# Padding two short contractions with zero rows so that they span as many partitions as their neighbours

## The chip, the cores and the metric

The kernel runs on one core of one Trainium2 chip. The metric is the device time of one execution in microseconds (us); the time of a kernel is the median of its runs. A profiled execution gives the trace, whose span (first to last instruction) is a little shorter than the device time of that execution. Engines: PE is TensorE's matmul stream, PEld its weight loads, DVE is VectorE, ACT is ScalarE, POOL is GpSimd, SP issues the DMAs.

## The reference

Eight batches of eight heads of attention, with 512 local tokens and 32 global tokens, feed a two-layer MLP with a Mish activation. Local queries see the globals and a window of 32 keys on either side; global queries see all keys.

```python
k_all = np.concatenate([k_g, k_l], axis=2)
v_all = np.concatenate([v_g, v_l], axis=2)
out_g = np.matmul(sm(scale * q_g @ k_all.T), v_all)
mask = np.abs(pos[:, None] - pos[None, :]) <= 32
s_l = np.concatenate([scale * q_l @ k_g.T, np.where(mask, scale * q_l @ k_l.T, -1e9)], axis=-1)
out_l = np.matmul(sm(s_l), v_all)
x = concatenate([out_g, out_l], axis=2).transpose(0, 2, 1, 3).reshape(B * S, H * D)
h = x @ w_in
return (h * np.tanh(softplus(h))) @ w_out
```

## The kernel before, in words

A unit of attention is one batch `b`, one pair of heads `hp` (4 pairs) and one tile `t` of 128 local queries (4 tiles), so there are 128 units. For a unit, `scores` (L595 to L607) multiplies queries with the keys of the window, `row_max` and `expo` make the softmax numerators, `p_hi` and `p_lo` split them into two half-precision parts in `ph`, and `p_turn` transposes `ph` by DMA into `pt`, in which the keys lie on the partitions. `pv` (L646) then multiplies `pt`, the stationary operand, with the values, the moving operand of 64 columns. Every product of two split numbers takes three matmuls (high with high, high with low, low with high). For each of two heads the keys come in two chunks: the first against `va`, the second against `vc`, so a unit has 2 x 2 x 3 = 12 matmuls into the tile `U`. How many keys (rows of both operands) a chunk has stands in the table `CHK`, by `t`: 96 and 96, 128 and 96, 128 and 96, 128 and 64.

The global queries are done once for each pair of heads, 32 times in all. `g_scores`, `g_max`, `g_exp`, `g_norm` and `g_turn` lead to the transposed numerators `gpt`; `g_pv` (L737) multiplies them in five chunks of keys with three matmuls each, 15 in all, into the tile `gu`. The first chunk holds the 32 globals, in the partitions 96 to 127 of `va` and `gpt`; the other four hold 128 local keys each, from `vf`.

`v_move` copies the split values from `vf` and `vgf` into `va` and `vc` by seven DMAs for each pair of heads. `vc` has two buffers of [96, 4, 2, 128]; its rows 64 to 95 are written for `t` 0 to 2 only. `ph` and `gph` are tiles that are kept over the whole program (`kept`, L264): POOL fills them with zeros at the start, and two or one of them are used in turn.

Beside attention runs the MLP: `m1_mm` (L787, tile `h`) and `m2_mm` (L855, tile `o`), with Mish and the split of its result (tiles `e`, `G`) on ACT and DVE between them. There are 17 blocks of 256 tokens with 8 steps each. `slot(u)` puts the work of one attention unit and of one MLP step together. At the start the weights are unpacked and scaled (`w_load`, `w_sum`, `w_stat`, `w_split`). The order of the instructions on each engine is set by the planner `Plan`, which simulates the tasks with given costs and takes, on each engine, the one that can begin first. The costs handed over for `pv` and `g_pv` are by counts and columns, `mm(12, 69)` and `mm(15, 69)`, not by rows.

Of the kernel before, what the change touches and what calls it, by code (L numbers as in the profile page):

```python
# [12 lines left out]
F16 = mybir.dt.float16  # L13
# [27 lines left out]


WIN = [(0, 192, 32), (128, 224, 0), (288, 224, 0), (448, 192, 0)]
CHK = [(96, 96), (128, 96), (128, 96), (128, 64)]
GC = 64


# [167 lines left out]
def attn_mish_kernel(ctx: ExitStack, tc: tile.TileContext, qt, kt, qt0, kt0, vm, vg, qg, w1, w2, consts_in, out, w64):  # L215
    nc = tc.nc
    V, A, T, G = nc.vector, nc.scalar, nc.tensor, nc.gpsimd
# [16 lines left out]
    X = pl.tile  # L234

    def rings(pool, *table):
        for tag, bufs, shape, dt in table:
# [8 lines left out]

          ("qs", 2, [128, 2, SL], F32R), ("ks", 2, [128, 2, KW], F32R), ("kl", 2, [128, 2, KW], F32R),
          ("qgh", 2, [128, 3, HP, 64], F32R), ("vgf", 2, [128, 2, 128], F16),
          ("vf", 2, [128, 4, 2, 128], F16), ("va", 2, [128, 4, 2, 128], F16), ("vc", 2, [96, 4, 2, 128], F16),

          ("P", 3, [128, 2, 224], F32), ("nm", 6, [128, 1], F32), ("sums", 3, [128, 4, 2], F32), ("rs", 2, [128, 4, 2], F32),
          ("pt", 2, [128, 8, 128], F16), ("x", 1, [128, 4, 2, 64], F32), ("xs", 1, [128, 2, 4, 128], F16),
# [9 lines left out]
          ("u", 1, [128, 4, 2, 64], F32))  # L262


    def kept(tag, bufs, shape):
        tiles = [const.tile(shape, F16, name=f"{tag}{n}") for n in range(bufs)]
        for x in tiles:
            G.memset(x, 0.0)
        pl.ring(tag, bufs, lambda name, it=itertools.cycle(tiles): next(it))

    kept("ph", 2, [128, 2, 2, 256])
    kept("gph", 1, [64, 2, 640])


    def mm(n, cols):
        return n * max(27, cols / 2.4)
# [25 lines left out]
    def scaled(e, dst, src, c):  # L302

        if e == ACT:
            A.activation(out=dst, in_=src, func=AF.Copy, scale=c)  # L305
        else:
            V.tensor_scalar(dst, src, c, None, ALU.mult)  # L307
# [270 lines left out]
    def bank(name):  # L578

        return [("h" if early else "sc", name)]  # L580
# [66 lines left out]
    def pv(b, hp, t):  # L647
# [3 lines left out]
        def go():  # L651
            for h in range(2):
                n = 0
                for c, vx in ((0, va), (1, vc)):
                    k = CHK[t][c]
                    for p, vl in ((0, 0), (0, 1), (1, 0)):
# [78 lines left out]
    def g_pv(b, hp):  # L735
        pt, vf, va, u = ("gpt", b, hp), ("vf", b, hp), ("va", b, hp), ("gu", b, hp)

        def go():
            n = 0
            for c in range(5):  # L740
                r = slice(0, 128) if c else slice(96, 128)
                vv = X[vf][:, c - 1] if c else X[va][r, 1]
                for p, vl in ((0, 0), (0, 1), (1, 0)):
                    T.matmul(X[u][:, :64], vv[:, vl, :], X[pt][r, p * 5 + c, :], start=(n == 0), stop=(n == 14))  # L744
                    n += 1
        pl.add(PE, mm(15, 69), go, r=[pt, vf, va], new=bank(u))
        for h in range(2):
            r = slice(64 * h, 64 * h + 64)
            pl.add([(ACT, 200), (DVE, 158)], 0, lambda e, r=r, h=h: scaled(e, xg[r, hp, b * SG:(b + 1) * SG], X[u][r, 32 * h:32 * h + 32],
                                                                          X["sv", b][r, 2:3]), r=[u, ("sv", b)], w=[["xg", (b, hp, h)]])  # L750
# [305 lines left out]
    for x in ORDER.split():  # L1056
        a, n = x[0], int(x[1:] or 0)
# [87 lines left out]
```

## Time and profile before

| quantity | value |
|---|---|
| median of 3 runs | 1034.23 us (1033.37 to 1034.86) |
| profiled execution | 1032.9 us, span 1031.1 us |
| PE busy | 944.5 us, 92% of the span, 7906 matmuls |
| PEld busy | 670.3 us, 65% |
| ACT busy | 681.1 us, 66% |
| DVE busy | 665.0 us, 64% |
| POOL busy | 81.8 us, 8% |

The busy time is an average over three stages: the preparation of the weights together with the first units of attention, the long middle in which attention and the MLP run side by side, and the tail in which only the MLP is left. The time that a group of matmuls takes is read from the start of the group to the start of what follows, since the matmuls are pipelined and the duration of each is longer than its distance to the next.

### The profile page before, as it was taken

The numbers are of one execution on the slowest core, as the hardware profiler recorded it, in microseconds if no ns is written. First come the engines' busy times: TensorE is split into PE (matmuls) and PEld (weight loads), VectorE is DVE, ScalarE is ACT, GpSimd is POOL, SyncE is SP. The second block draws the span as 40 slices with busy tenths as digits, with TensorE's granted clock in tenths as the row PEclk, the third lists the DMA queues.
The fourth block names the chain that finished last, engine by engine and source line by source line (L and its number), as shares of the span: only waits on it lengthen the run. The fifth ranks groups of instructions, "written<-read, shape, count | busy, mean of one in ns | idle before, by whom it ended". The sixth has DMA issues, their size and how long they took to land.

```text
span 1031.1 us, 20578 instructions
## 1 busy us (share of the span) xinstructions
PE 944.5 (92%) x7906; PEld 670.3 (65%) x7906; DVE 665.0 (64%) x1704; ACT 681.1 (66%) x1321; POOL 81.8 (8%) x60
## 2 busy tenths in 40 slices
PE   3456797899999999999999999999999999999996
PEld 2234475566776777777767777777777777666663
DVE  6877896887667766776676666767676655422221
ACT  3465566666887788778878788787878788311110
POOL 2725222410000000000000000000000000000000
PEclk9999998999999999999999999999999999999998
DMA  9847983696758764766566665665576444100000
GB/s 333 220 115 171 281 233 78 121 187 155 165 105 176 144 143 105 182 141 141 116 163 148 131 131 129 159 128 133 119 162 125 116 75 79 38 11 21 1 21 21
DMA packets 231802, 134.65 MB, mean 131 GB/s; under 512 B 197528, under 2 KB 209048, under 8 KB 230680
## 3 DMA queue, kind: packets, MB, share of 16 engines
q1 hardware_dynamic: 231704, 133.34, 56.6%
q8 instruction: 62, 1.02, 0.4%
q14 instruction: 36, 0.29, 0.1%
HBM read 63.55 MB, written 8.91 MB: 70 GB/s over the span
## 4 chain that ended last, share of the span: by engine, by line
PE 71%; DVE 11%; DMA 7%; issue 2%; ACT 2%; SPq 1%; POOL 0%; ACTq 0%; DVEq 0%
PE o L855 29%; PE h L787 29%; PE U L657 4%; PE s L606 4%; DMA vraw<-in_vm 3%; PE g L695 2%; PE gu L744 2%; DMA gpt<-gph 2%; DVE vmx L479 1%; DMA pt<-ph 1%; DVE ph L640 1%; DVE P L612 1%; DVE ks L300 1%; DVE kl L544 1%; DMA wraw<-in_w 1%
## 5 line engine op out<-in xcount | busy, mean ns | idle before, releaser
L855 PE MATMUL o<-W,G 128*128 128x512 f16 x1632 | 389.9, 379 | 0.0
L787 PE MATMUL h<-xh,W 128*128 128x256 f16 x2048 | 379.3, 275 | 5.2 <-ACT e L830 5.1
L787 PEld LDWEIGHTS <-W 128*128 128x128 f16 x3264 | 310.9, 98 | 69.8 <-issue 5.5
L787 PE MATMUL h<-xl,W 128*128 128x256 f16 x1024 | 281.0, 274 | 0.0
L855 PEld LDWEIGHTS <-G 128*128 128x128 f16 x1632 | 156.8, 98 | 144.3 <-issue 0.3
L830 ACT ACTIVATE e<-h,c 128x512 f32<-128x512 f32 (+1 forms) x137 | 92.6, 683 | 117.0 <-PE h L787 115.9
L621 ACT ACTIVATE P<-P,nm 128x192 f32<-128x192 f32 (+1 forms) x256 | 117.8, 460 | 40.3 <-DVE nm L612 39.0
L612 DVE CUSTOM_DVE_ANT_0 P<-s,consts 128x192 f32<-128x192 f32 (+1 forms) x256 | 90.1, 367 | 79.3 <-PE s L606 70.2
L307 DVE TENSOR_SCALAR G<-e,c 128x512 f16<-128x512 f32 x129 | 63.2, 490 | 115.3 <-ACT e L830 115.1
L640 DVE SCALAR_TENSOR_TENSOR ph<-P,ph 128x384 f16<-128x384 f32 (+1 forms) x128 | 79.1, 619 | 82.0 <-ACT ph L305 81.3
L843 DVE SCALAR_TENSOR_TENSOR G<-e,c,G 128x512 f16<-128x512 f32 (+1 forms) x137 | 102.0, 744 | 3.4
L830 ACT ACT_TABLE_LOAD x79 | 101.4, 1283 | 1.4
L621 ACT ACT_TABLE_LOAD x74 | 94.9, 1283 | 1.4
L657 PEld LDWEIGHTS <-pt 96*128 96x128 f16 (+2 forms) x1536 | 64.1, 101 | 34.2 <-DMA pt<-ph 21.6
L305 ACT ACTIVATE ph<-P 128x384 f16<-128x384 f32 (+1 forms) x128 | 69.7, 547 | 16.3 <-DMA pt<-ph 13.2
L657 PE MATMUL U<-va,pt 128*128 128x64 f16 (+1 forms) x768 | 62.0, 200 | 14.8 <-DMA pt<-ph 12.5
L606 PE MATMUL s<-ks,qs 128*128 128x192 f32 (+1 forms) x216 | 71.4, 353 | 1.4 <-DVE qs L536 0.8
L657 PE MATMUL U<-vc,pt 96*128 96x64 f16 (+1 forms) x768 | 61.3, 198 | 0.0
L393 POOL TENSOR_TENSOR W<-W,wr 128x512 int32<-128x512 int32 x32 | 50.2, 1579 | 77.3 <-DVE W L391 42.4
L716 ACT ACTIVATE gP<-g,gmx 64x288 f32<-64x288 f32 x64 | 30.4, 476 | 37.8 <-DVE gmx L711 37.6
L606 PE MATMUL s<-kl,qs 128*128 128x192 f32 (+1 forms) x216 | 54.2, 274 | 0.0
L403 PE MATMUL ws<-W 128*128 128x128 bf16 x128 | 17.7, 285 | 37.0 <-POOL W L393 37.0
(102 smaller groups left out, 1016.6 us busy)
## 6 DMA issues: line engine op xcount, KB each, us to landing
kraw<-in_kt SPq DMA_DIRECT2D x27, 640.0 KB, 4.7
qraw<-in_qt SPq DMA_DIRECT2D x27, 512.0 KB, 4.1
W<-in_w SPq DMA_DIRECT2D x19, 512.0 KB, 6.1
out<-ob SPq DMA_DIRECT2D x34, 256.0 KB, 2.6
vraw<-in_vm SPq DMA_DIRECT2D x8, 1024.0 KB, 6.1
wraw<-in_w SPq DMA_DIRECT2D x13, 512.0 KB, 6.2
vc<-vf SPq DMA_DIRECT2D x32, 128.0 KB, 2.3
va<-vf SPq DMA_DIRECT2D x32, 96.0 KB, 2.3
```

The lines of the kernel that those rows point to most:

```text
L305: A.activation(out=dst, in_=src, func=AF.Copy, scale=c)
L307: V.tensor_scalar(dst, src, c, None, ALU.mult)
L393: pl.add(POOL, pool(512), lambda: G.tensor_tensor(f(), f(), X["wr", k], ALU.add), r=[("wr", k)], w=[key])
L606: T.matmul(X[s][:, :w], X[qs][:, h, t * 128:(t + 1) * 128], X[k][:, h, c0:c0 + w], start=(i == 0), stop=(i == 1))
L612: pl.add(DVE, 69 + 1.04 * w, lambda: V.tensor_tensor_reduce(out=X[P][:, h, :w], in0=X[s][:, :w], in1=mask[:, m0:m0 + w], scale=-SCALE, sca ...
L621: pl.add(ACT, 160 + 0.832 * w + 93, lambda: A.activation(out=X[P][:, h, :w], in_=X[P][:, h, :w], func=AF.Exp, bias=X[nm], scale=-1.0, accu ...
L640: pl.add(DVE, dve(n), lambda: V.scalar_tensor_tensor(p_part(X[ph], t, 1), p_src(X[P], t), PSC, p_part(X[ph], t, 0), ALU.mult, ALU.subtract ...
L657: T.matmul(X[u][:, t, h, :], X[pt][:k, p * 4 + h * 2 + c, :], X[vx][:k, t, vl, h * 64:(h + 1) * 64], start=(n == 0), stop=(n == 5))
L787: T.matmul(X[h][:, f * TB:(f + 1) * TB], wh(i, wl)[:, off:off + 128], X[x][:, d, o:o + TB], start=(n == 0), stop=(n == 11))
L830: chain(blk, i, ACT, 571, lambda a, z: A.activation(out=X[e][:, a:z], in_=hv(blk, i)[:, a:z], func=AF.Mish, bias=0.0, scale=X[c][:, 0:1]), ...
L843: chain(blk, i, DVE, 602, lambda a, z: V.scalar_tensor_tensor(gp(1, blk, i)[:, a:z], X[e][:, a:z], X["c", blk][:, 2:3], gp(0, blk, i)[:, a ...
L855: T.matmul(X[o], gp(g, blk, i)[:, f, t * 128:(t + 1) * 128], wh(8 + i, wl)[:, f * 512:(f + 1) * 512], start=(i == 0 and n == 0), stop=(i = ...
```

## The change

The second chunk of the last query tile has 96 rows in place of 64, and the globals' chunk of `g_pv` has 128 rows in place of 32. For the first, the two buffers of `vc` become kept tiles which POOL fills with zeros at the start: rows 64 to 95 of the last query tile's part are never written by a DMA and stay zero. For the second, the columns 0 to 95 of `gph`, which stay zero, become the rows 0 to 95 of the first chunk of `gpt`, and they multiply whatever values stand in those rows of `va`.

```diff
-CHK = [(96, 96), (128, 96), (128, 96), (128, 64)]
+CHK = [(96, 96), (128, 96), (128, 96), (128, 96)]
...
-          ("vf", 2, [128, 4, 2, 128], F16), ("va", 2, [128, 4, 2, 128], F16), ("vc", 2, [96, 4, 2, 128], F16),
+          ("vf", 2, [128, 4, 2, 128], F16), ("va", 2, [128, 4, 2, 128], F16),
...
     kept("ph", 2, [128, 2, 2, 256])
+    kept("vc", 2, [96, 4, 2, 128])
     kept("gph", 1, [64, 2, 640])
...
             for c in range(5):
-                r = slice(0, 128) if c else slice(96, 128)
-                vv = X[vf][:, c - 1] if c else X[va][r, 1]
+                vv = X[vf][:, c - 1] if c else X[va][:, 1]
                 for p, vl in ((0, 0), (0, 1), (1, 0)):
-                    T.matmul(X[u][:, :64], vv[:, vl, :], X[pt][r, p * 5 + c, :], start=(n == 0), stop=(n == 14))
+                    T.matmul(X[u][:, :64], vv[:, vl, :], X[pt][:, p * 5 + c, :], start=(n == 0), stop=(n == 14))
```

The order of the instructions on PE, DVE, ACT and SP is the same in both kernels, and so is their number. On POOL two instructions are new, at the start of the program. This is what stands there before; `ph` and `gph` are the kept tiles, and `p` is the result of the first reduction over the partitions, for the scale of the values:

```order
L268 MEMSET ph_72 128x1024
L268 MEMSET ph_73 128x1024
L268 MEMSET gph_76 64x1280
L490 ISA
L490 ISA p_0_151<-vmx_123 128x1
L393 ISA
```

And this is what stands there in the changed kernel, at the same place on POOL:

```order
L269 MEMSET ph_72 128x1024
L269 MEMSET ph_73 128x1024
L269 MEMSET vc_76 96x1024
L269 MEMSET vc_77 96x1024
L269 MEMSET gph_80 64x1280
L492 ISA
L492 ISA p_0_155<-vmx_127 128x1
L395 ISA
```

The two fills of `vc` stand behind those of `ph` and ahead of that of `gph` and of the first reduction.

## Rows read from the trace of the kernel before

**Rows 1.** The page, busy time, share of the span and instructions of each engine.
```profile
PE 944.5 (92%) x7906; PEld 670.3 (65%) x7906; DVE 665.0 (64%) x1704; ACT 681.1 (66%) x1321; POOL 81.8 (8%) x60
```

**Rows 2.** Busy time by stage: stretch, its length, engines' busy us, granted clock, DMA.
```profile
0.00:211.00 211.00, 138.56 (x1029) 92.81 (x1030) 164.08 (x373) 120.67 (x259) 79.46 (x54) 0.98 0.74 192
211.00:886.00 675.00, 670.81 (x5959) 487.54 (x5957) 466.14 (x1272) 536.50 (x1028) 2.32 (x6) 1.00 0.63 136
886.00:1031.00 145.00, 135.16 (x922) 89.92 (x919) 34.80 (x61) 23.90 (x35) 0.00 (x0) 0.98 0.05 17
```

**Rows 3.** What PE waited for from 211 us on: total, times, longest.
```profile
PE U L657 <- DMA pt<-ph: 2.6, 6, 0.8
PE gu L744 <- DMA gpt<-gph: 0.8, 2, 0.6
```

**Rows 4.** Timeline of PE, a unit with chunks of 128 and 96 rows.
```profile
500.86 0.25 PE L657 MATMUL U<-va,pt 128*128 128x64 f16 x3
500.95 0.25 PE L657 MATMUL U<-vc,pt 96*128 96x64 f16 x3
...
501.22 0.42 PE L695 MATMUL g<-ks,qgh 128*64 128x256 f32 x2
```

**Rows 5.** Timeline of PE, a unit with chunks of 128 and 64 rows.
```profile
513.52 0.26 PE L657 MATMUL U<-va,pt 128*128 128x64 f16 x3
513.72 0.26 PE L657 MATMUL U<-vc,pt 64*128 64x64 f16 x3
513.91 0.26 PE L657 MATMUL U<-va,pt 128*128 128x64 f16 x3
...
514.29 0.28 PE L787 MATMUL h<-xh,W 128*128 128x256 f16 x1
```

**Rows 6.** Timeline of PE around the product of the global queries.
```profile
508.45 1.46 PE L855 MATMUL o<-W,G 128*128 128x512 f16 x6
509.75 0.27 PE L787 MATMUL h<-xh,W 128*128 128x256 f16 x1
...
511.06 1.46 PE L855 MATMUL o<-W,G 128*128 128x512 f16 x6
512.45 0.26 PE L744 MATMUL gu<-gpt,va 32*128 32x64 f16 x3
512.64 0.52 PE L744 MATMUL gu<-gpt,vf 128*128 128x64 f16 x12
```

**Rows 7.** Groups by shape: 64-row matmuls, and weight loads of 96 rows.
```profile
L657 PE MATMUL U<-vc,pt 64*128 64x64 f16 x192 | 17.1, 198 | 0.0
...
L657 PEld LDWEIGHTS <-pt 96*128 96x128 f16 x768 | 36.0, 102 | 7.3 <-DMA pt<-ph 5.5 <-issue 1.0
```

**Rows 8.** Timeline of PE, 64-row groups: first from 211 us on, and last.
```profile
230.18 0.26 PE L657 MATMUL U<-vc,pt 64*128 64x64 f16 x3
...
885.36 0.26 PE L657 MATMUL U<-vc,pt 64*128 64x64 f16 x3
```

**Rows 9.** Line L744 by stage: stretch, length, PE and PEld busy us.
```profile
211.00:886.00 675.00, 18.51 (x390) 14.17 (x390) 1.00 0.63 136
```

**Rows 10.** The chain that ended last, first stage: start us, us, what.
```profile
85.64 0.64 PE U L657 x12
...
123.32 1.17 PE U L657 x12
...
166.65 8.18 PE h L787 x48
...
182.63 0.66 PE U L657 x12
```

**Rows 11.** Timeline of POOL at the start: start us, us, what, idle before.
```profile
0.72 1.84 POOL L268 MEMSET ph<- 128x1024 f16 x2 [0.29 <-POOLq L1134]
...
13.32 0.65 POOL L490 PARTITION_ALL_REDUCE p<-vmx  x1 [9.66 <-DVE vmx L485]
```

**Rows 12.** Busy time from 166 to 170 us; the number behind POOL's is the granted clock.
```profile
166.00:170.00 4.00, 3.35 (x16) 2.31 (x16) 3.22 (x6) 3.94 (x7) 0.00 (x0) 0.50 0.42 97
```

## The prediction

> **What bounds the kernel now.** I read the engines' busy times first. PE is busy for 944.5 us of 1031.1, well ahead of ACT with 681.1 and DVE with 665.0 [rows 1]. That is an average, so I split the span into stages. Up to 211 us PE is busy for only 138.56 of 211 us, while DVE has 164.08: here the weights are prepared, and PE is not the limit. From 211 to 886 us PE is busy for 670.81 of 675 us, against 536.50 for ACT and 466.14 for DVE [rows 2]. From 886 us on only the MLP is left; 135.16 of 145 us are PE's, and no line that the change touches runs there. So in the middle stage a microsecond taken from PE should be a microsecond of the end, if PE does not have to wait for something in its place. The view of waits says how near that is: from 211 us on PE waited 2.6 us in six places for the transposed numerators `pt`, and 0.8 us in two for `gpt`, never longer than 0.8 us [rows 3]. It is thus tightly fed, with a few places where it is already a little early.
>
> Next I read the timeline of PE at the matmuls which the change touches, and took the time from one start to the next. A busy engine may still be stalled inside, and here it is. A unit whose chunks have 128 and 96 rows starts at 500.86 and its successor at 501.22: 0.36 us for 12 matmuls, 0.09 us for each group of three, and the step from 128 to 96 rows costs nothing [rows 4]. A unit of the last query tile has the same 12 matmuls with the same 64 columns, but runs from 513.52 to 514.29: 0.77 us. Each group of three takes 0.19 or 0.20 us there [rows 5]. The extra 0.10 us comes once in each group, at 128 to 64 and at 64 to 128 rows alike. The 32-row chunk of the globals shows the same: six `o` matmuls take 1.30 us when `h` follows (508.45 to 509.75) but 1.39 us when the 32-row chunk follows (511.06 to 512.45); then its three matmuls take 0.19 us up to the 128-row ones [rows 6]. So there is a stall of about 0.10 us on each change between a short contraction (64 or 32 rows) and a long one (96 or 128), on an engine that counts as busy.
>
> **The change, part by part.**
>
> The last query tile's second chunk gets 96 rows. No matmul is added or removed; the unit becomes the one of the 128- and 96-row groups, so its four stalls go: 0.77 - 0.36 = 0.41 us. There are 192 matmuls of 64 rows, six to a unit, so 32 units [rows 7]. Of these 27 lie in the middle stage, from 230.18 to 885.36 us [rows 8]. That makes 27 x 0.41 = 11.1 us.
>
> The globals' chunk gets 128 rows. Its two stalls go: 1.39 - 1.30 = 0.09 us before it, and 0.19 - 0.09 = 0.10 us behind, with the 0.09 us for three long matmuls from the unit above. In the middle stage 390 matmuls of that line run, which is 26 products of 15 [rows 9]: 26 x 0.19 = 4.9 us. In two of them PE waited for `gpt` just before [rows 3], and the stall ahead lies inside that wait; 2 x 0.09 = 0.2 us come off. That leaves 4.7 us.
>
> The other five units and six products fall into the first stage. There a unit on the chain takes 0.64 us in one place and 1.17 us in another, and the latter has 64-row groups, so up to 0.53 us are in it [rows 10]. All of them together would be at most 5 x 0.53 + 6 x 0.19 = 3.8 us, and nothing is the lower end, since DVE is the busier engine there. On the chain I find two of these units, at 123.32 and 182.63 us (0.53 and 0.41 us at most) and take 0.7 us, three quarters of these two, since the chain leaves PE for DVE soon after each.
>
> Against this stand new waits in the middle stage. PE gets 0.41 us ahead of ACT, DVE and the transposes at each such unit, and where one of them has less slack than that, a part comes back as a wait. The eight waits now seen are 3.4 us together. The others have the room to follow: ACT's 536.50 us in 675 would become 536.50 in 659, or 81%. I put the loss at 0.8 us, a quarter of the waits now seen; its bounds are nothing and the half of the gain, which is a rival below.
>
> The two fills of `vc` on POOL have the width of those of `ph`, which take 1.84 us for two. They stand ahead of the fill of `gph` and the first reduction. That reduction starts at 13.32 us after 9.66 us of idleness, in which POOL waits for DVE [rows 11], so the fills lie in that idleness and 7.8 us of it are left. If that cover were gone, 1.84 us would move down to the first scale of the values, in a stage where PE has slack. I count nothing. The DMAs into `vc` now also wait for these fills, which end long before the first values exist. The reads of all rows of `va` add no wait in the middle stage: the unit of the second query tile, which runs before the globals' product, has read all the same rows already.
>
> The sum: 11.1 + 4.7 + 0.7 - 0.8 = 15.7 us. The profiled execution took 1032.9 us with a span of 1031.1, so its span should fall to 1015.4 and its time to 1017.2. The median of the runs shown is 1034.23, 1.3 us above the profiled one, and gives **1018.5 us**.
>
> Padding to 96 rows might also make weight loads more expensive, so I weigh that. A load of 96 rows takes 102 ns [rows 7], yet three matmuls of 96 rows with their three loads take 0.09 us between 128-row ones [rows 4]; so loads overlap with matmuls and with each other on the same rows. [...]
>
> **The rivals.**
>
> *Half of the gain is absorbed.* PE runs ahead, and at the boundaries of the batches, where PE already waits for `pt`, or behind the globals' products, where it waits for `gpt`, the waits grow. For it: the eight waits exist, and ACT has 79% of the stage. Against it: each is at most 0.8 us, and what they wait for starts from PE's own scores a few us before, mostly with no touched unit in between. Half of 15.8 us lost gives 1034.2 - 7.9 - 0.7, about 1026 us.
>
> *All of the first stage counts too.* 11.1 + 4.7 + 3.8 = 19.6 us, without losses: 1014.6 us. Against it: DVE's load up to 211 us.
>
> *The change does nothing measurable.* If the stall belonged not to the number of rows but to the operands (a change of tile from `va` to `vc`), it would stay: 1034 us. But `va` to `vc` in a unit with 128 and 96 rows shows none [rows 4].
>
> [...]
>
> [...]
>
> **How the numbers follow.** Within 0.2% (2.1 us) is what a measurement of this kernel can hardly tell from no change. Chances: my sum (1016 to 1021 us) 0.77; the larger gain (about 1014.6) 0.08; half absorbed (about 1026) 0.10; no change 0.02; the lost clock 0.02; the loads 0.01. The first three are faster by over 0.2%: 0.95. Same: 0.02, slower: 0.03. The range runs from 1015.0 to 1022.5, which holds the first case with its bounds, a loss of up to 4 us, and part of the larger gain.
>
> **What would show it.** In the changed trace the shapes of 64 and 32 rows are gone from `U` and `gu`; the last query tile's units take 0.36 us from the first start to the next instruction, and the globals' products 0.45 us (15 at the pace of 12 in 0.36), with six `o` matmuls ahead of them back at 1.30 us. The stage up to the last unit of attention ends some 15 us sooner, the tail keeps its 145 us, and PE's waits from 211 us on stay below 5 us together. POOL's first reduction still starts near 13.3 us. I would be wrong if the units stay at 0.77 us, if the waits for `pt` and `gpt` take what the stalls gave, or if the first stage moves by more than 2 us either way, since its idle times depend on the phase of many queues.

## The result, and the profile after

The changed kernel takes 1020.42 us in the median of four runs (1018.93 to 1021.21) against 1033.8 us before (four runs; the three of the table above have 1034.23), a ratio of 0.9862 with a 95% interval of 0.9845 to 0.9879. Measured again beside the later experiments it took 1021.41 us against 1033.64, a ratio of 0.9883 (0.9866 to 0.9900). The forecast was 1018.5 us, with a range from 1015.0 to 1022.5. The profiled execution is the fastest of the four: 1018.93 us, with a span of 1017.1 us against 1031.1.

The page of the changed kernel, busy time and share of the span of each engine:

```profile
PE 925.7 (91%) x7906; PEld 664.6 (65%) x7906; DVE 668.5 (66%) x1704; ACT 680.9 (67%) x1321; POOL 82.2 (8%) x62
```

PE has the same number of instructions and is busy for 18.8 us less than in [rows 1]; part of this, 4.8 us, came back as idle time (91.4 us of the span against 86.6). The windows show where it went. Middle stage and tail of the changed kernel, with the border moved to the end of its attention (columns as in [rows 2]):

```profile
211.00:872.00 661.00, 655.16 (x5957) 482.49 (x5956) 465.43 (x1272) 535.55 (x1028) 2.31 (x6) 1.00 0.64 139
872.00:1017.00 145.00, 135.16 (x922) 89.92 (x919) 34.93 (x61) 23.91 (x35) 0.00 (x0) 0.98 0.05 17
```

The tail is that of [rows 2] to the hundredth, 135.16 us of PE with 922 matmuls in 145 us, and the middle stage has become 14 us shorter. Within it the timeline of PE shows the two places of [rows 5, 6] after the change:

```profile
505.51 1.46 PE L856 MATMUL o<-W,G 128*128 128x512 f16 x6
506.80 0.25 PE L745 MATMUL gu<-gpt,va 128*128 128x64 f16 x3
506.89 0.51 PE L745 MATMUL gu<-gpt,vf 128*128 128x64 f16 x12
507.24 0.35 PE L608 MATMUL s<-ks,qs 128*128 128x224 f32 x1
...
507.76 0.26 PE L659 MATMUL U<-va,pt 128*128 128x64 f16 x3
507.86 0.25 PE L659 MATMUL U<-vc,pt 96*128 96x64 f16 x3
507.95 0.25 PE L659 MATMUL U<-va,pt 128*128 128x64 f16 x3
508.04 0.25 PE L659 MATMUL U<-vc,pt 96*128 96x64 f16 x3
508.13 0.27 PE L788 MATMUL h<-xh,W 128*128 128x256 f16 x1
```

The unit of the last query tile takes 0.37 us (507.76 to 508.13) where it took 0.77. The six `o` matmuls take 1.29 us (505.51 to 506.80), as with an `h` behind them, and the globals' product takes 0.44 us from its first start to the next `s`. The stalls are gone at both places. What came back is in the view of waits, from 211 us on (total, times, longest):

```profile
PE U L659 <- DMA pt<-ph: 4.1, 6, 1.8
PE gu L745 <- DMA gpt<-gph: 1.3, 4, 0.4
```

That is 5.4 us against 3.4 in [rows 3], and over the 5 us that the prediction gave as a bound. On POOL the two fills of `vc` and the first reduction stand as follows (start, duration, idle time before):

```profile
2.49 1.84 POOL L269 MEMSET vc<- 96x1024 f16 x2
...
13.55 0.65 POOL L492 PARTITION_ALL_REDUCE p<-vmx  x1 [8.12 <-DVE vmx L487]
```

The reduction begins 0.23 us later than in [rows 11] and still waits 8.12 us for DVE: the fills are covered.

### The profile page after: what moved, and what is told of

It is laid out like the page before. It is cut to its first block, busy times and chain, and to the rows that moved or that the text cites. A ratio compares the mean times of both kernels' runs of the same rounds, so it can differ in the third digit from the quotient of the medians.

```text
span 1017.1 us, 20581 instructions
## 1 busy us (share of the span) xinstructions
PE 925.7 (91%) x7906; PEld 664.6 (65%) x7906; DVE 668.5 (66%) x1704; ACT 680.9 (67%) x1321; POOL 82.2 (8%) x62
## 4 chain that ended last, share of the span: by engine, by line
PE 65%; DVE 12%; DMA 8%; ACT 4%; issue 3%; SPq 1%; POOL 0%; ACTq 0%; DVEq 0%
PE o L856 28%; PE h L788 26%; PE s L608 4%; PE U L659 3%; DMA vraw<-in_vm 3%; DMA pt<-ph 2%; PE g L697 2%; DMA gpt<-gph 2%; PE gu L745 1%; DVE vmx L481 1%; DVE P L614 1%; DVE ph L642 1%; DVE G L309 1%; SPq L296 1%; DVE kl L546 1%
## 5 line engine op out<-in xcount | busy, mean ns | idle before, releaser
L659 PEld LDWEIGHTS <-pt 96*128 96x128 f16 (+1 forms) x1536 | 59.3, 101 | 33.5 <-DMA pt<-ph 26.9
L659 PE MATMUL U<-va,pt 128*128 128x64 f16 (+1 forms) x768 | 59.4, 199 | 19.7 <-DMA pt<-ph 19.7
L659 PE MATMUL U<-vc,pt 96*128 96x64 f16 x768 | 58.7, 198 | 0.0
```

What stands on the lines that cost most here:

```text
L659: T.matmul(X[u][:, t, h, :], X[pt][:k, p * 4 + h * 2 + c, :], X[vx][:k, t, vl, h * 64:(h + 1) * 64], start=(n == 0), stop=(n == 5))
```

## The experiments

Theory A is the one of the prediction: a stall of about 0.10 us on PE at each change between a contraction of 64 or 32 rows and one of 96 or 128. Its rivals: the stall belongs to the operands, or to the short matmuls themselves. A second question came up with the result: why less than the sum arrived.

**One part at a time.** First the last query tile alone. The edit, against the changed kernel:

```diff
-                vv = X[vf][:, c - 1] if c else X[va][:, 1]
+                r = slice(0, 128) if c else slice(96, 128)
+                vv = X[vf][:, c - 1] if c else X[va][r, 1]
...
-                    T.matmul(X[u][:, :64], vv[:, vl, :], X[pt][:, p * 5 + c, :], start=(n == 0), stop=(n == 14))
+                    T.matmul(X[u][:, :64], vv[:, vl, :], X[pt][r, p * 5 + c, :], start=(n == 0), stop=(n == 14))
```

> Only the 64-row chunk of the last query tile is padded to 96 rows; the globals' chunk keeps its 32 rows. Theory A (a stall of 0.10 us at each change between a short contraction of 64 or 32 rows and a long one of 96 or 128): the 27 units of the middle stage give 27 x 0.41 = 11.1 us, less about 1 us of grown waits, so 10 us below the kernel before, about 1024 us; the globals' product keeps 0.19 us for its first three matmuls. Theory B (the stall belongs to the change from va to vc, or to anything else but rows): no change, 1034 us.

Measured: 1027.45 us against 1033.05, ratio 0.9941 (0.9925 to 0.9958). That is 5.6 us, about half of what was expected. The globals' product kept its stall, as the timeline of PE shows:

```profile
511.06 0.26 PE L746 MATMUL gu<-gpt,va 32*128 32x64 f16 x3
511.25 0.52 PE L746 MATMUL gu<-gpt,vf 128*128 128x64 f16 x12
```

More than half of the missing part lies in PE's waits from 211 us on:

```profile
PE U L659 <- DMA pt<-ph: 4.2, 6, 1.3
PE gu L746 <- DMA gpt<-gph: 2.4, 5, 0.8
```

6.6 us against 3.4 in [rows 3]: 3.2 us of the gain came back as waits, not the 1 us that was allowed for. The table in the next section has the rest.

Then the globals' chunk alone, again against the changed kernel:

```diff
-CHK = [(96, 96), (128, 96), (128, 96), (128, 96)]
+CHK = [(96, 96), (128, 96), (128, 96), (128, 64)]
```

> Only the globals' chunk is padded to 128 rows (and vc is kept and filled with zeros, unused); the 64-row chunk stays. Theory A: 26 products x 0.19 = 4.9 us, less what turns into waits for the transposed numerators gpt right before (in the changed kernel five such waits of 0.27 to 0.37 us, where there were two before), so 3 to 4 us below the kernel before, about 1030 us. Rival (the globals' stalls are wholly hidden in that wait): no change.

Measured: 1029.96 us against 1033.05, ratio 0.9966 (0.9953 to 0.9979), 3.1 us: as theory A had it. (The waits for `gpt` in the changed kernel that the expectation names are four by the view above, not five.)

**Half of the changes, with the same matmuls.** The edit, in `pv` of the kernel before:

```diff
-                for c, vx in ((0, va), (1, vc)):
+                for c, vx in ((0, va), (1, vc))[::1 - 2 * h]:
```

> The kernel before with its row counts, but the second head of each unit takes its vc chunk first and its va chunk second: the same 12 matmuls with the same rows, in the order va, vc, vc, va. A unit of the last query tile then has two changes between 128 and 64 rows in place of four. Theory A: it takes 0.36 + 2 x 0.10 = 0.56 us in place of 0.77, and 27 x 0.21 = 5.6 us go, less a small part in waits: about 1029 us. Theory B1 (each 64-row group of three is slow in itself): 0.77 us stays, 1034 us. Theory B2 (a change of the tile from va to vc costs): the same half would go, but units with 96 rows would gain too, which they cannot, since their groups already take 0.09 us.

The timeline of PE, a unit of the last query tile:

```profile
515.94 0.26 PE L657 MATMUL U<-va,pt 128*128 128x64 f16 x3
516.13 0.34 PE L657 MATMUL U<-vc,pt 64*128 64x64 f16 x6
516.41 0.26 PE L657 MATMUL U<-va,pt 128*128 128x64 f16 x3
516.51 0.27 PE L787 MATMUL h<-xh,W 128*128 128x256 f16 x1
```

It takes 0.57 us with six matmuls of 64 rows in it, where [rows 5] had 0.77 us with the same six. So short matmuls are not slow in themselves; the number of changes sets the price, 0.10 us each. The time fell to 1030.45 us, ratio 0.9975 (0.9964 to 0.9986): 2.6 us and not 5.6. The profile has a reason for it: PE waited 3.6 us for `gpt` and 2.9 us for `pt` from 211 us on, about twice what it did before, and the stretch between the first and the last 64-row unit of the middle stage [rows 8] is 1.9 us shorter, about 5 us of stalls less 3.1 us of grown waits. The profiled execution is the slowest of the ten, though, at 1033.26 us, so this shows the waits and not the size of the median.

**More changes.** The edit, in the kernel before, which leaves 32 keys of each such tile out of the result:

```diff
-CHK = [(96, 96), (128, 96), (128, 96), (128, 64)]
+CHK = [(96, 96), (128, 96), (128, 64), (128, 64)]
```

> The kernel before with a second short chunk: the third query tile's second chunk takes 64 rows in place of 96 too (it leaves out 32 keys of that tile). Theory A: its 32 units now take 0.77 us in place of 0.36, 27 or 28 of them in the middle stage: 11 us more than before, about 1045 us. If fewer rows cost nothing in themselves and the time of the last query tile's units had another cause: 1034 us.

Measured: 1044.08 us against 1033.05, ratio 1.0101 (1.0078 to 1.0123), 11.0 us more with less to compute. The timeline of PE, a unit of the third query tile:

```profile
514.60 0.26 PE L657 MATMUL U<-va,pt 128*128 128x64 f16 x3
514.79 0.26 PE L657 MATMUL U<-vc,pt 64*128 64x64 f16 x3
...
515.36 0.28 PE L787 MATMUL h<-xh,W 128*128 128x256 f16 x1
```

It now takes 0.76 us as well. The operands are the same tiles as in the units of 0.36 us, so the number of rows decides.

**How much padding is enough.** The changed kernel with 64 rows in the globals' chunk (`slice(64, 128)` in the edit shown first), beside the changed kernel itself on the same chip:

> The changed kernel once more, beside the next three on the same chip. About 1019 to 1021 us, 13 us below the kernel before. Theory A: each unit of the last query tile gives 0.41 us and each globals' product 0.20 us in the profile, whatever the first stage does in this execution.

> The changed kernel, but the globals' chunk takes 64 rows (64 to 127) in place of 128. Theory A (64 rows are short, as 32 are): the two stalls of the globals' product stay, 0.19 us to the first 128-row matmul, so no gain from them, about 4 us slower than the changed kernel and equal to the run with the units alone, 1024 to 1027 us. Rival (the stall grows with the number of missing rows): half of the gain, 2 us slower than the changed kernel.

Measured: 1021.41 us for the changed kernel and 1026.9 us (1025.33 to 1031.11) with 64 rows, ratios 0.9883 (0.9866 to 0.9900) and 0.9938 (0.9921 to 0.9955) to the kernel before. The timeline of PE with 64 rows:

```profile
513.57 1.46 PE L857 MATMUL o<-W,G 128*128 128x512 f16 x6
514.96 0.26 PE L746 MATMUL gu<-gpt,va 64*128 64x64 f16 x3
515.15 0.52 PE L746 MATMUL gu<-gpt,vf 128*128 128x64 f16 x12
```

1.39 us for the six `o`, 0.19 us for the first three matmuls: exactly the 32-row chunk of [rows 6]. Padding that stops at 64 rows buys nothing: the stall is the same for 32 and for 64 rows.

**Where the rest of the gain went.** PE's waits at `pt` and `gpt`, 3.4 us before, grew whenever stalls of the units were taken out: to 5.4 us in the changed kernel, 6.6 us with the units alone, 6.5 us with two changes; without the globals' stalls alone they stayed, at 3.5 us. Two additions to the planner were tried. It gets a table `lag` of times by which a task may begin later than its inputs allow; the first addition enters 3 us for the maxima of the values (DVE reads `vraw`, the loaded values, for them), the second 1.2 us for the globals' product. The edit of both, against the changed kernel:

```diff
-                t = max([done[d] + ... for d in deps] + [start[a] for a in after] + [0])
+                t = max([done[d] + ... for d in deps] + [start[a] for a in after] + [0]) + self.lag.get(n, 0)
...
                    r=[("vraw", b)], new=() if hp else [("vmx", m)], w=[[m, hp]])
+            if b > 1:
+                pl.lag[len(pl.tasks) - 1] = 3000
...
         pl.add(PE, mm(15, 69), go, r=[pt, vf, va], new=bank(u))
+        if b:
+            pl.lag[len(pl.tasks) - 1] = 1200
```

The first alone:

> The changed kernel, but the planner is told that the maxima of the values can begin 3 us later, from the third batch on, so that DVE does not stand before them while the load of the values is still under way. Theory C (what the change lost in the middle stage is waits at the boundaries of the batches, where DVE stands before the values and the transposed numerators pt come late): DVE's wait for vraw falls from 11.6 to under 4 us, PE's wait for pt from 211 us on from 4.1 to under 2 us, and 2 to 3 us are gained, about 1017.5 us. Rival (the waits come from the transposes' own time in the DMA queue): PE's waits stay at 4 to 5 us, no change from the changed kernel.

> The changed kernel with the first addition alone once more, beside the second alone on the same chip, since its first measurement had a wide interval. Theory D: no better than the changed kernel, 1020 to 1021 us, PE's wait for pt at about 4 us though DVE no longer stands before the values. Rival: 1018 us.

Measured: 1019.7 us (0.9847 to 0.9889) and, again, 1019.3 us (0.9841 to 0.9888); the changed kernel has 0.9862 and 0.9883, so no gain is to be told. DVE's wait for `vraw` over the whole span fell from 11.6 to 0.7 us, as meant, yet PE's wait for `pt` stayed at 4.2 us, and at 5.7 us in the second profile. Theory C, that DVE standing before the values makes `pt` late, falls. The chain of the first of these two profiles shows what PE waits for (start, duration, what):

```profile
306.49 0.58 SPq L297
...
307.18 6.58 DMA pt<-ph
313.76 0.05 issue
313.81 0.53 PE U L662 x12
```

The transpose took 6.58 us, where the median of the 128 is 3.1 us: SP issued it right behind the 1 MB load of the values (the SPq row). PE waited for `pt` at four more places of this profile, up to 418.22, 522.22, 626.24 and 730.09 us, for 0.28 to 1.07 us (timeline of PE). In the changed kernel the transposes issued right behind the loads of 514.65, 618.73 and 723.38 us took 6.3 to 6.5 us to land, where the median of its 128 is 3.1 us too (view of the tile `pt`). That the load is why they are late was read from these places and not tried by itself.

Both additions, the second alone, and both without the padding:

> As the run before it, and the planner is also told that the globals' product can begin 1.2 us later than its numerators are planned to land, from the second batch on. Theory C: PE's wait for gpt from 211 us on goes from 1.3 us to under 0.5 us, one more microsecond than in the run before it, about 1016.5 us. Rival: the wait moves to another place (pt, or the scores), no gain over the run before it.

> The changed kernel with the second addition to the planner alone: the globals' product can begin 1.2 us later than its numerators are planned to land; the maxima of the values stay where they were. Theory D (the waits of PE are for transposes that take longer than planned, and giving PE other work ahead of the globals' product fills them; DVE's standing before the values costs nothing): PE's waits from 211 us on fall below 2.5 us and the time comes near that with both additions, 1014 to 1016 us. Rival (both are needed, each fills its own places): the waits for gpt go, those for pt stay at about 4 us, 1018 to 1020 us.

> The kernel before, with both additions to the planner (maxima of the values 3 us later, globals' product 1.2 us later) but without the padding. Theory A+C (the stalls and the waits add up, and with the waits gone the padding gives its whole sum): some 15.8 us slower than the run with padding and both additions, about 1029 us, 4 to 5 us below the kernel before. Rival (the additions help only a kernel whose PE runs early, since the waits come from the padding): no gain without the padding, 1033 us.

> The changed kernel with both additions once more, beside the run without padding on the same chip: 1012.5 to 1014 us, PE's waits from 211 us on below 2 us.

| kernel | median us | ratio to before (95%) |
|---|---|---|
| padding, both additions | 1013.28 | 0.9802 (0.9787 to 0.9816) |
| the same, second measurement | 1014.02 | 0.9809 (0.9787 to 0.9830) |
| padding, globals' product later | 1016.41 | 0.9826 (0.9812 to 0.9839) |
| no padding, both additions | 1028.53 | 0.9948 (0.9929 to 0.9967) |

With the second addition alone PE's waits for the transposes nearly vanish, and one other wait is left (from 211 us on):

```profile
PE h L791 <- ACT e L834: 2.1, 1, 2.1
PE U L660 <- DMA pt<-ph: 0.6, 3, 0.2
PE gu L746 <- DMA gpt<-gph: 0.2, 1, 0.2
```

With padding and both, second measurement, this row is all:

```profile
PE U L662 <- DMA pt<-ph: 0.5, 1, 0.5
```

Theory D, that other work ahead of the globals' product fills PE's waits, is borne out for the waits: 0.8 us is left of those for the transposes. The time of 1016.41 us is 0.4 us above what it gave, and whether the first addition adds anything to the second is not settled, since the intervals of 0.9826 and 0.9802 overlap. Nor is it shown how the second addition does it. It moves other instructions too: at the batch near 514 us SP issues the transpose 0.69 us behind the load of the values in the changed kernel and 2.74 us behind it with the second addition alone (timeline of SP, one after the other):

```profile
514.65 0.58 SPq L296 DMA_DIRECT2D vraw<-in_vm  x1
515.34 1.23 SPq L467 DMA_TRANSPOSE pt<-ph  x1
```

```profile
512.71 0.58 SPq L297 DMA_DIRECT2D vraw<-in_vm  x1
515.45 1.23 SPq L468 DMA_TRANSPOSE pt<-ph  x1
```

The additions also give more than the waits in these views: without padding 4.8 us, while the waits for the transposes fell from 3.4 to 1.2 us. Where the rest comes from stays open.

With both additions in place the padding is worth 1028.53 - 1014.02 = 14.5 us. Padding with both additions is the fastest kernel of this study.

## Why the prediction was right, step by step

The forecast held, and so did its mechanism. Its sum of 15.7 us came out 2.3 us above the 13.4 us of the medians, for three terms: the units were counted one too many (0.4 us), the new waits were put too low (1.2 us), and the term of the first stage could not be known.

The stall at each change of rows: right. It was read from [rows 4 to 6], and the run with two changes, the one with more short chunks and the one with 64 rows bear it out, at 0.10 us each and for 64 rows as for 32.

The units: the saving of each is right, about 0.40 us, but the count is off by one. The groups by shape of the kernel before, from 211 us on, have this line:

```profile
L657 PE MATMUL U<-vc,pt 64*128 64x64 f16 x156 | 13.4, 193 | 0.0
```

156 matmuls, six to a unit, are 26 units and not 27; six lie in the first stage and not five. The term is 26 x 0.41 = 10.7 us in place of 11.1, and the forecast would have been 1018.9 us. The globals' products, 26 in the middle stage, are counted rightly.

How much of this arrived can be read between two places that every kernel has. The first matmuls against `vc` of the last query tile from 211 us on, and the last ones, stood at 230.18 and 885.36 us [rows 8], 655.18 us apart. In the timelines of the changed kernel, of the units alone and of the globals alone they stand here:

```profile
229.57 0.26 PE L659 MATMUL U<-vc,pt 96*128 96x64 f16 x3
...
871.48 0.25 PE L659 MATMUL U<-vc,pt 96*128 96x64 f16 x3
```

```profile
230.54 0.26 PE L659 MATMUL U<-vc,pt 96*128 96x64 f16 x3
...
879.23 0.25 PE L659 MATMUL U<-vc,pt 96*128 96x64 f16 x3
```

```profile
231.76 0.26 PE L659 MATMUL U<-vc,pt 64*128 64x64 f16 x3
...
882.30 0.26 PE L659 MATMUL U<-vc,pt 64*128 64x64 f16 x3
```

Between them lie 24 whole units, six of the eight stalls of the two at the ends, and 25 globals' products. By the prediction's figures that is 24 x 0.41 + 6 x 0.10 = 10.4 us for the units and 25 x 0.19 = 4.8 us for the globals.

| stretch of | length us | shorter by | stalls gone | waits grown |
|---|---|---|---|---|
| the kernel before | 655.18 | | | |
| the changed kernel | 641.91 | 13.3 | 15.2 | 2.0 |
| the units alone | 648.69 | 6.5 | 10.4 | 3.2 |
| the globals alone | 650.54 | 4.6 | 4.8 | 0.1 |

Stalls less grown waits give what arrived, within 0.1 us in two rows and within 0.7 us for the units alone. With both additions to the planner the same stretch is 649.77 us without padding and 634.07 us with it, 15.7 us apart: 15.0 us of stalls, with 24 globals' products between the two places, and 0.7 us of waits.

The new waits: the term that was too small. It had 0.8 us, and PE's waits for the transposes grew by 2.0 us. The place was named rightly, the boundaries of the batches and the globals' products. The size was taken as a quarter of the waits then seen, which does not bound a wait that PE walks into by being earlier: the longest went from 0.8 to 1.8 us.

That the two parts give 5.6 + 3.1 = 8.7 us by themselves and 13.4 together is 4.7 us, and the profiles account for it: 2.2 us in the stretch above (6.5 + 4.6 against 13.3), of which 1.3 us are waits, and 2.6 us ahead of it, where the first place came 0.4 and 1.6 us later with one part and 0.6 us earlier with both.

The first stage: 0.7 us was taken, and the profile shows 0.3 us at its end, but this stage is not the same from one execution to the next. The first unit that starts behind 221 us, row by row for the kernel before, the changed kernel, and the one with the globals' chunk alone (timeline of PE):

```profile
221.58 0.25 PE L657 MATMUL U<-va,pt 128*128 128x64 f16 x3
```

```profile
221.28 0.25 PE L659 MATMUL U<-va,pt 128*128 128x64 f16 x3
```

```profile
223.37 0.25 PE L659 MATMUL U<-va,pt 128*128 128x64 f16 x3
```

The third has two stalls fewer at each globals' product than the first and is 1.8 us later. The two profiles with the first addition alone, one kernel, have this unit at 222.28 and at 220.94 us, and PE's wait for the DMA into `pt` ahead of one and the same unit of this stage is 2.70 us in the first (up to 111.49 us) and 1.35 us in the second (up to 109.97 us). A term of 0.7 us could not be tested here; that the stage came out within 0.4 us of it is luck.

The fills on POOL: right, nothing, with 8.12 us of cover left against the 7.8 forecast. The rivals: absorption came, for 2.0 of 15.2 us in the stretch above and not for half; with the units alone it was 3.2 of 10.4 us, nearer to that rival. The lost clock and the loads, to which the chances give 0.02 and 0.01, were the author's estimates, and the middle stage shows a loss by neither: its granted clock is 1.00 before and after, a load of 96 rows takes 98 ns in the mean there, before and after (groups by shape, 211 to 886 and 211 to 872 us), and three matmuls of 96 rows with their loads take 0.09 us in the changed kernel as in [rows 4].

## What to carry to other kernels

On a busy PE, take the time from one start to the next and compare groups that differ in one thing: a short contraction between long ones cost 0.10 us on the way in and 0.10 us on the way out here, more than the three matmuls themselves, and zero rows up to the neighbours' 96 or 128 took it away. Where padding is not possible, put the short ones next to each other: that halved the stalls of a unit here, 0.77 us to 0.57. Then look for what the faster engine walks into. The waits that came back took 2.0 us of the gain here and 3.2 us with the units alone, and a planner that was told that the globals' product and the maxima of the values can begin later took most of them away, from 5.4 us to 1.8 and 0.5 us in two profiles. And count the places in the trace: one unit too many was 0.4 us of the sum.

## What was not expected of the hardware

From 90 to 120 us the granted clock did not tell PE's pace here. It is 1.00 in the kernel before and 0.51 in the changed one (windows, before and then changed):

```profile
90.00:120.00 30.00, 18.04 (x140) 11.61 (x139) 22.28 (x66) 15.80 (x45) 8.63 (x5) 1.00 0.98 233
```

```profile
90.00:120.00 30.00, 17.85 (x143) 11.90 (x143) 23.15 (x66) 15.41 (x44) 6.56 (x5) 0.51 0.97 227
```

Yet a group of three matmuls against `vc` takes 0.16 us there in both, as the timelines show, before and then changed:

```profile
102.38 0.35 PE L657 MATMUL U<-vc,pt 96*128 96x64 f16 x3
102.54 0.35 PE L657 MATMUL U<-va,pt 128*128 128x64 f16 x3
```

```profile
101.79 0.35 PE L659 MATMUL U<-vc,pt 96*128 96x64 f16 x3
101.95 0.35 PE L659 MATMUL U<-va,pt 128*128 128x64 f16 x3
```

In the middle stage it is 0.09 us. So PE kept the same pace at this place in both, slower than that of the middle stage, though one profile reads 1.00 and the other 0.51. The mean clock of the two profiles (0.994 before, 0.973 after) is no sign of a difference.
